# A new order of the pieces of a step, a one-lane last layer and a split output half in a two-layer recurrent kernel

## The chip, the cores and the metric

One core of one Trainium2 chip runs the whole program. The metric is device time in microseconds (us), lower is better. Engines: PE is TensorE's matmuls, PEld its weight loads, DVE VectorE, ACT ScalarE, SP the queue that issues weight DMAs. A "step" below is one pass of the kernel's main loop. The "granted clock" is the share of TensorE's full clock that the profile reports as granted: 1.00 is full, 0.50 half.

## The reference, cut to what matters

```python
def _A_ref(x, mem0, Wq, Wk, Wv, Wo, seg_len):       # 32 heads of 192, model width 640
    mem = mem0                                       # 8 memory rows
    for s in range(n_seg):                           # 64 segments of 32 rows
        h = concat([mem, x[segment s]])              # 40 rows
        q, k, v = h @ Wq, h @ Wk, h @ Wv
        o = softmax(mask(q k^T * scale)) v @ Wo
        mem = o[:, :8]                               # feeds the next segment
        outs.append(o[:, 8:])
def _B_ref(x, wqkv, wo):                             # local attention, 32 heads of 20, window 8, dilation 2
    ...
x = x + A(layernorm(x)); x = x + B(layernorm(x))     # and the same two layers once more
x = x + A(layernorm(x)); x = x + B(layernorm(x))
```

Layer A is recurrent: the memory rows of a segment must be there before the projections of the next one can be made.

## The kernel before

The kernel runs segment t of the first A layer (lane 0) and segment t-2 of the second A layer (lane 1) side by side, so a matmul has 2 x 40 = 80 columns. Steps 0 and 1 have only lane 0, steps 2 to 63 both, steps 64 and 65 only lane 1. Layer B of the step before is woven in. After the last step the list `LAST` does layer B of the last rows alone.

`ORDER` is the order of the pieces in a step. Each engine takes its own pieces in that order. What the argument needs: `K Q V` projections, `S` scores, `E` their exponential (ScalarE), `EM` their mask (VectorE), `PO` attention output in PSUM, `R` reciprocal sums (ScalarE), `OT1 OT2` normalised outputs (VectorE), `Oa Ob` halves of the output projection, `O7x/y/z` the eighth one in three parts; the digit is the quad of heads. `by byE` end layer B and write the next step's input. `LSQ` (VectorE: a square, two reductions, a high and a low part), `lst` (two statistics matmuls), `LMV LR LAP` are the next step's layernorm, `MEMa MEMb` copy the memory rows.

```python
ORDER = """
K0 Q0 bsq K0y QE0 KE0 V0 bst bmv VE0 Q1 S0 K1 T0 QE1 br bap E0 ...
... by byE R5 K7 KE7 V7 S7 VE7 OT15 E7 OT25 LSQ PO6 EM7 Oa2 R6 T7 Ob2 Oa3 TE7
Ob3 OT16 OT26 Oa5 PO7 Oa6 R7 lst LMV Ob5 Oa4 Ob6 OT17 LR OT27 Ob4 LAP O7x O7y MEMa O7z MEMb X1
""".split()
LAST = """
bsq bst bmv br bap bq bqE bk bkE bs0 be0 bv bs1 be1 eb0 bvE bt eb1 btE bp0 on0 bp1 on1 bo boE by byE
""".split()

    def ln_sq(self, x):                                                     # LSQ and bsq
        sq = self.bp.tile([P, NC, NX], BF16, name="sq", tag="sq")
        nc.vector.tensor_tensor(out=sq[:], in0=x[:], in1=x[:], op=ALU.mult)
        s = self.bp.tile([P, 2, NX], F32, name="ln_s", tag="xc")
        for j, v in enumerate((x, sq)):
            nc.vector.tensor_reduce(out=s[:, j, :], in_=v[:].rearrange("p c n -> p n c"), op=ALU.add, ...)
        hl = ...                                                            # part of sq
        nc.vector.tensor_copy(out=hl[:, 0], in_=s[:])
        nc.vector.tensor_tensor(out=hl[:, 1], in0=s[:], in1=hl[:, 0], op=ALU.subtract)
        return hl

    def ln_stats(self, hl):                                                 # lst and bst
        for j in range(2):
            nc.tensor.matmul(ps[:, 0:2 * NX], lhsT=self.ones[:], rhs=hl[:, j]..., start=(j == 0), stop=(j == 1))

    def ln_big(self, x, mr, dst):                                           # LAP and bap
        nc.vector.tensor_tensor(out=xc[:], in0=x[:], in1=m..., op=ALU.subtract)
        for l in range(2):
            nc.vector.tensor_tensor(out=dst[:, :, l, :], in0=xc[...], in1=r..., op=ALU.mult)

    def b_proj(self, part, name):                                           # bq and bk: 64 columns, two lanes
        for n in range(NC):
            for c in range(NC):
                nc.tensor.matmul(ps[:, NX * n:NX * (n + 1)], lhsT=self.wqkv[:, part, c, P * n:P * (n + 1)], rhs=h[:, c, :], ...)
```

The softmax here doesn't subtract the row's maximum and nothing guards it: scores larger than these inputs give would overflow.

Of the kernel before, what the change touches and what calls it, by code (L numbers as in the profile page):

```python
# [12 lines left out]
ACT = mybir.ActivationFunctionType  # L13
ALU = mybir.AluOpType
# [3 lines left out]
P = 128  # L18
# [26 lines left out]


ORDER = """
K0 Q0 bsq K0y QE0 KE0 V0 bst bmv VE0 Q1 S0 K1 T0 QE1 br bap E0 TE0 KE1 V1 S1 EM0 Q3 PO0 VE1 QE3 E1 bq T1 R0 K2
KE2 bqE TE1 Q2 K3 V2 QE2 OT10 S2 KE3 bk EM1 OT20 S3 PO1 VE2 E2 bkE Q4 T2 EM2 bs1 E3 QE4 V3 R1 K4 TE2 be1 VE3
Q5 OT11 OT21 KE4 PO2 R2 EM3 T3 eb1 bs0 be0 V4 QE5 Oa0 VE4 bv TE3 OT12 OT22 bvE Q6 S4 PO3 eb0 E4 bt R3 QE6 btE  # L50
K5 T4 EM4 K6 KE5 TE4 bp0 V5 OT13 Ob0 OT23 KE6 on0 S5 bp1 VE5 PO4 T5 Oa1 E5 R4 on1 TE5 V6 bo Q7 EM5 OT14 S6 boE
OT24 VE6 Ob1 E6 QE7 PO5 T6 EM6 TE6 by byE R5 K7 KE7 V7 S7 VE7 OT15 E7 OT25 LSQ PO6 EM7 Oa2 R6 T7 Ob2 Oa3 TE7
Ob3 OT16 OT26 Oa5 PO7 Oa6 R7 lst LMV Ob5 Oa4 Ob6 OT17 LR OT27 Ob4 LAP O7x O7y MEMa O7z MEMb X1
""".split()


LAST = """
bsq bst bmv br bap bq bqE bk bkE bs0 be0 bv bs1 be1 eb0 bvE bt eb1 btE bp0 on0 bp1 on1 bo boE by byE
""".split()

def half_order():

    order = []
    for n in ORDER:
        if n[0] in "KQV" and len(n) == 2:
            order += [(n[0].lower(), int(n[1]), 0), (n[0].lower(), int(n[1]), 1)]
        elif n[:2] in ("Oa", "Ob"):
            order.append(("o", int(n[2]), int(n[1] == "b")))
        elif n == "O7x":
            order += [("o", 7, 0), ("o", 7, 1)]  # L70
    assert len(set(order)) == len(order) == 8 * NQUAD
    return order

def half_blocks(kind, i, h):

    if kind == "o":
        if i == NQUAD - 1:
            blocks = [(m, c) for c in range(NC) for m in O_ROWS[0] + O_ROWS[1]]
        else:
            blocks = [(m, c) for rows in O_ROWS for m in rows for c in range(NC)]  # L80
    elif (kind, i) == ("k", 0):
        blocks = [(c, n) for c in range(NC - 1) for n in range(6)] + [(NC - 1, n) for n in range(6)]
    else:
        blocks = [(c, n) for n in range(6) for c in range(NC)]
    return blocks[15 * h:15 * (h + 1)]
# [4 lines left out]
def resident_pieces():  # L90

    at, t = {}, 0.0
    for n in ORDER:
        if n[0] in "KQV" and len(n) == 2 and n != "K0":
            at.update({(n[0].lower(), int(n[1]), h): t + 15 * h for h in range(2)})
        elif n == "K0":
            at.update({("k", 0, h): t + 15 * h for h in range(2)})
        elif n[:2] in ("Oa", "Ob"):
            at[("o", int(n[2]), int(n[1] == "b"))] = t
        elif n == "O7x":  # L100
            at.update({("o", 7, h): t + 15 * h for h in range(2)})
        t += 30 if len(n) == 2 and n[0] in "KQV" else 15 if n[0] == "O" and n[1] in "ab" else 30 if n == "O7x" else NO_WEIGHTS.get(n.rstrip("01234567"), 0)
    pieces = [(at[u] + 8 * q, u + (q,)) for u in half_order() for q in range(2)]
    pieces.sort()
    stream, n_s = set(), len(pieces) - N_RES
    k = 0
    for j in range(n_s):
        want = (j + 0.5) * t / n_s
        while k < len(pieces) - (n_s - j) and abs(pieces[k + 1][0] - want) <= abs(pieces[k][0] - want):
            k += 1  # L110
        stream.add(pieces[k][1])
        k += 1
    return {u for _, u in pieces} - stream

class Kernel:
    def __init__(self, ctx, tc, xT, m0T, wA, wqkv, wo, out):

        self.tc = tc
        self.nc = tc.nc
        self.x = xT  # L120
        self.mem0 = m0T
        self.wA = wA
        self.b_src = (wqkv, wo)
        self.out = out
        self.n_seg = 2 * xT.shape[0]
        pool = lambda name, bufs, **kw: ctx.enter_context(tc.tile_pool(name=name, bufs=bufs, **kw))
        self.cp = pool("consts", 1)
        self.wres = pool("wres", 1)
        self.wring = pool("wring", RING)
        self.ap1 = pool("act1", 1)  # L130
        self.ap2 = pool("act2", 2)
        self.bp = pool("bact", 1)
        self.xp = pool("xio", 1)
        self.ps_one = pool("ps_one", 1, space=PSUM)
        self.units = {}
        self.place = {u: n for n, u in enumerate(half_order())}
        self.resident = resident_pieces()
        self.cur = {}
        self.n_big = 0
        self.xt, self.ots, self.qxs, self.kp, self.qp, self.vp, self.tp = {}, {}, {}, {}, {}, {}, {}  # L140
        self.x_load(0)
        self.build_consts()
# [148 lines left out]
    def span_of(self, t):  # L291

        self.l0 = 0 if t < self.n_seg else 1
        self.l1 = 2 if t >= LAG else 1
        self.cs = slice(LT * self.l0, LT * self.l1)

    def proj(self, ps, kind, i, h, t, chained=False):

# [131 lines left out]
    def a_o7(self, part):  # L430

        for k in {"x": range(18), "y": range(18, 24), "z": range(24, 30)}[part]:
            self.o_mm(NQUAD - 1, k // 15, k % 15)

    def acc_lanes(self, g):

        return self.acc[g][:, 0:(3 - g) * NT].rearrange("p (c l n) -> p c l n", l=2, n=LT)
# [18 lines left out]
    def ln_sq(self, x):  # L456

        nc = self.nc
        sq = self.bp.tile([P, NC, NX], BF16, name="sq", tag="sq")
        nc.vector.tensor_tensor(out=sq[:], in0=x[:], in1=x[:], op=ALU.mult)  # L460
        s = self.bp.tile([P, 2, NX], F32, name="ln_s", tag="xc")
        for j, v in enumerate((x, sq)):
            nc.vector.tensor_reduce(out=s[:, j, :], in_=v[:].rearrange("p c n -> p n c"), op=ALU.add, axis=mybir.AxisListType.X)
        hl = sq[:].rearrange("p c n -> p (c n)")[:, 0:4 * NX].rearrange("p (j a n) -> p j a n", j=2, a=2)
        nc.vector.tensor_copy(out=hl[:, 0], in_=s[:])
        nc.vector.tensor_tensor(out=hl[:, 1], in0=s[:], in1=hl[:, 0], op=ALU.subtract)
        return hl

    def ln_stats(self, hl):
        nc = self.nc  # L470
        ps = self.big("ps_st")
        for j in range(2):
            nc.tensor.matmul(ps[:, 0:2 * NX], lhsT=self.ones[:], rhs=hl[:, j].rearrange("p a n -> p (a n)"), start=(j == 0), stop=(j == 1))  # L473
        return ps

    def ln_mv(self, ps):

        nc = self.nc
        m = self.bp.tile([P, NX], F32, name="ln_m")
        nc.vector.tensor_scalar(out=m[:], in0=ps[:, 0:NX], scalar1=1.0 / D, scalar2=None, op0=ALU.mult)  # L480
        v = self.bp.tile([P, NX], F32, name="ln_v")
        nc.vector.tensor_tensor(out=v[:], in0=m[:], in1=m[:], op=ALU.mult)
        nc.vector.scalar_tensor_tensor(out=v[:], in0=ps[:, NX:2 * NX], scalar=1.0 / D, in1=v[:], op0=ALU.mult, op1=ALU.subtract)
        return m, v

    def ln_r(self, mv):

        nc = self.nc
        m, v = mv
        nc.scalar.activation(out=v[:], in_=v[:], func=ACT.Ln, bias=self.eps_t[:])  # L490
        r = self.bp.tile([P, NX], F32, name="ln_r")
        nc.scalar.activation(out=r[:], in_=v[:], func=ACT.Exp, scale=-0.5)
        return m, r

    def ln_big(self, x, mr, dst):
# [1 line left out]
        nc = self.nc  # L497
        m, r = mr
        xc = self.bp.tile([P, NC, NX], F32, name="ln_xc", tag="xc")
        nc.vector.tensor_tensor(out=xc[:], in0=x[:], in1=m[:].unsqueeze(1).to_broadcast([P, NC, NX]), op=ALU.subtract)  # L500
        for l in range(2):
            nc.vector.tensor_tensor(out=dst[:, :, l, :], in0=xc[:, :, SEG * l:SEG * (l + 1)],
                                    in1=r[:, SEG * l:SEG * (l + 1)].unsqueeze(1).to_broadcast([P, NC, SEG]), op=ALU.mult)

# [22 lines left out]
    def b_kE(self, b):  # L527

        o = SEG * (b % 2)
        for l in range(2):  # L530
            k = self.bkp[:, 0:NC * NX].rearrange("p (c l n) -> p l c n", c=NC, l=2)[:, l]
            self.nc.vector.tensor_tensor(out=self.KX[:, :, l, :, o:o + SEG], in0=k.unsqueeze(2).to_broadcast([P, NC, 2, SEG]),
                                         in1=self.par_mask[:].unsqueeze(3).to_broadcast([P, NC, 2, SEG]), op=ALU.mult)
# [1 line left out]
    def b_qE(self):  # L535

        self.qx = self.bp.tile([P, NC, BPC, NX], BF16, name="QX", tag="xc")
        q = self.bqp[:, 0:NC * NX].rearrange("p (c n) -> p c n", c=NC)
        self.nc.vector.tensor_tensor(out=self.qx[:], in0=q.unsqueeze(2).to_broadcast([P, NC, BPC, NX]),
                                     in1=self.pair_mask[:].unsqueeze(3).to_broadcast([P, NC, BPC, NX]), op=ALU.mult)  # L540

    def b_v(self):
        nc = self.nc
# [195 lines left out]
    def a_piece(self, n, t):  # L739
        if n == "K0":  # L740
            return self.k0(t)
        if n == "K0y":
            return self.k0y()
        if n[:2] == "O7":
            return self.a_o7(n[2])
        if n == "X1":
            return self.b_x1(t)
        k, i = n[:-1], int(n[-1])
# [12 lines left out]
    def step(self, t):  # L761
# [3 lines left out]
        nt = t + 1  # L765
        if a:
            self.span_of(t)
        if 1 < nt < self.n_seg:
            self.x_take(nt)
        for n in ORDER if a else LAST:  # L770
# [82 lines left out]
```

## Time and profile before

| stage (profiled run, 3138.8 us) | us |
|---|---|
| start to the end of step 0 | 89.9 |
| step 1 | 48.2 |
| steps 2 to 63, two lanes | 2890.2 |
| shortest / median of these | 46.43 / 46.44 |
| step 64; step 65 up to the last output matmul | 43.7; 45.9 |
| tail: start of the last output matmul to the end of the last sum | 18.4 |
| landing of the output | 2.6 |

A step is counted from the start of its first key matmul to that of the next step. Two-lane steps are 92% of the time.

The busy times by window (each engine's busy us, its instructions in brackets, then TensorE's granted clock, the DMA share and GB/s) in the middle of the run, kernel before:

```profile
core 0: us, PE busy (x) PEld busy (x) DVE busy (x) ACT busy (x) POOL busy (x), PEclk, DMA share, GB/s
1500.00:1600.00 100.00, 99.93 (x2721) 99.59 (x2718) 77.33 (x220) 57.13 (x123) 0.83 (x2) 1.00 0.86 264
```

The timeline of VectorE in the kernel before, around the pieces that make the statistics (columns: start, busy us, engine, line, operation, out<-in, shapes, count):

```profile
1529.21 0.33 DVE L460 TENSOR_TENSOR sq<-xin_86 128x320 bf16<-128x320 bf16 x1
1529.46 0.70 DVE L463 TENSOR_REDUCE ln_s<-xin_86 128x64 f32<-128x320 bf16 x1
1530.08 0.70 DVE L463 TENSOR_REDUCE ln_s<-sq 128x64 f32<-128x320 bf16 x1
1530.81 0.23 DVE L465 CAST sq<-ln_s 128x128 bf16<-128x128 f32 x1
1531.08 0.29 DVE L466 TENSOR_TENSOR sq<-ln_s,sq 128x128 bf16<-128x128 f32 x1
...
1536.29 0.49 DVE L500 TENSOR_TENSOR ln_xc<-xin_86,ln_m 128x320 f32<-128x320 bf16 x1
1536.88 0.56 DVE L502 TENSOR_TENSOR hT_90<-ln_xc,ln_r 128x160 bf16<-128x160 f32 x2
1537.36 0.20 DVE L454 CAST hT_90<-ps_acc_51495 128x48 bf16<-128x48 f32 x1
```

LSQ is the five operations from 1529.21 to 1531.37. The timeline of TensorE in the same kernel:

```profile
1534.09 0.28 PE L473 MATMUL ps_st<-sq,ones 128*128 128x128 bf16 x2
...
1537.17 0.42 PE L420 MATMUL ps_acc_51496<-OT,w_o_11_1962 128*128 128x80 bf16 x7
1537.61 0.45 PE L303 MATMUL ps_k<-hT_90,w_k_00_386 128*128 128x80 bf16 x8
```

The statistics matmuls come 2.7 us after their operands.

The chain of waits of the kernel before in the tail (start, length, engine, tile, line, count):

```profile
3122.83 1.51 PE ps_bq L523 x25
...
3124.36 1.49 DVE QX L539
3125.85 0.41 DVE KX_373 L532
...
3126.30 0.47 PE ps_bs L575 x5
...
3126.79 0.59 ACT EB_142 L581
```

Three further exponentials of 0.59 us follow. Everything in this stretch is serial.

### The profile page before, as it was taken

How to read it: one execution, taken by the hardware profiler on the slowest of the kernel's cores; microseconds unless marked ns; L12 is line 12 of the kernel's file. 1: busy time of each engine (PE TensorE's matmuls, PEld its weight loads, DVE VectorE, ACT ScalarE, POOL GpSimd, SP SyncE). 2: the span in 40 equal slices, each digit the busy share in tenths (PEclk: the TensorE clock that was granted, in tenths of full speed). 3: DMA queues.
4: the chain of work that ended last, by engine and by line, in shares of the span. 5: the costliest groups of instructions: out<-in, count | busy, mean ns of one | idle time of the engine just before them, and what ended most of it. 6: DMA issues, size and time to landing. Idle time of an engine off the chain costs nothing.

```text
span 3138.8 us, 185804 instructions
## 1 busy us (share of the span) xinstructions
PE 3063.2 (98%) x83160; PEld 3036.4 (97%) x83160; DVE 2358.2 (75%) x6883; ACT 1747.2 (56%) x3829; POOL 48.2 (2%) x162
## 2 busy tenths in 40 slices
PE   6899999999999999999999999999999999999996
PEld 5799999999999999999999999999999999999996
DVE  3577777777777777777777777777777777777775
ACT  2355556555556556556555655555655655655653
POOL 2000000000000000000000000000000000000000
PEclk6899999999999999999999999999999999999998
DMA  9988888888888888888888888888888888888885
GB/s 360 320 263 267 263 262 265 264 264 265 266 268 263 268 266 263 268 266 263 268 266 261 267 263 267 261 265 268 263 267 266 264 267 267 263 269 266 262 274 184
DMA packets 487807, 838.02 MB, mean 267 GB/s; under 512 B 54240, under 2 KB 261984, under 8 KB 487008
## 3 DMA queue, kind: packets, MB, share of 16 engines
q1 hardware_dynamic: 477648, 820.89, 83.2%
q8 instruction: 651, 10.67, 1.4%
q10 hardware_dynamic: 9360, 5.26, 0.6%
q14 instruction: 148, 1.21, 0.1%
HBM read 823.31 MB, written 2.62 MB: 263 GB/s over the span
## 4 chain that ended last, share of the span: by engine, by line
PE 95%; DMA 3%; issue 1%; DVE 1%; ACT 0%; SPq 0%; DVEq 0%; ACTq 0%
PE ps_k L303 18%; PE ps_q L303 18%; PE ps_v L303 18%; PE ps_vt L349 6%; PE ps_o L401 5%; PE ps_s L368 5%; PE ps_by L634 2%; PE ps_bq L523 2%; PE ps_bv L548 2%; PE ps_bk L523 2%; DMA w_ring<-in_wA_dram 1%; PE ps_bs L575 1%; PE ps_bo L598 1%; PE ps_bvt L561 1%; PE ps_st L473 0%
## 5 line engine op out<-in xcount | busy, mean ns | idle before, releaser
L303 PEld LDWEIGHTS <-w_ring 128*128 128x128 bf16 x17754 | 784.4, 100 | 19.4 <-DMA w_ring<-in_wA_dram 10.5
L388 ACT ACTIVATE R<-ps_o 64x320 f32<-64x320 f32 (+1 forms) x1056 | 448.5, 425 | 273.8 <-PE ps_o L401 223.6
L342 ACT CAST VT_140<-ps_v 128x480 bf16<-128x480 f32 (+1 forms) x528 | 288.9, 547 | 230.7 <-PE ps_v L303 227.6
L329 ACT CAST KF_121<-ps_k 128x480 bf16<-128x480 f32 (+1 forms) x264 | 144.1, 546 | 391.2 <-PE ps_k L303 383.3
L374 ACT ACTIVATE Em<-ps_s 80x320 bf16<-80x320 f32 (+1 forms) x528 | 223.3, 423 | 157.2 <-PE ps_s L368 110.7
L420 PEld LDWEIGHTS <-w_ring 128*128 128x128 bf16 x6600 | 291.2, 100 | 3.5 <-DMA w_ring<-in_wA_dram 2.6
L335 DVE CAST QT_127<-ps_q 128x320 bf16<-128x320 f32 (+1 forms) x264 | 127.1, 481 | 203.4 <-PE ps_q L303 203.4
L357 DVE COPY Vt_134<-ps_vt 80x512 bf16<-80x512 bf16 x528 | 219.2, 415 | 71.5 <-PE ps_vt L349 69.3
L349 PE MATMUL ps_vt<-ident,VT_140 128*128 128x128 bf16 x3168 | 267.7, 221 | 0.0
L408 DVE TENSOR_TENSOR OT<-ps_o,R 128x320 bf16<-128x320 f32 (+1 forms) x528 | 249.9, 473 | 22.3 <-ACT R L390 16.6
L329 ACT CAST KF_123<-ps_k 128x480 bf16<-128x480 f32 (+1 forms) x264 | 144.1, 546 | 205.6 <-PE ps_k L303 203.9
L390 ACT ACTIVATE R<-R 128x320 f32<-128x320 f32 (+1 forms) x528 | 244.0, 462 | 16.6
L401 PE MATMUL ps_o<-Em,Vt_134 80*128 80x80 bf16 (+1 forms) x4224 | 238.0, 199 | 1.4 <-issue 1.3
L335 DVE CAST QT_125<-ps_q 128x320 bf16<-128x320 f32 (+1 forms) x264 | 126.5, 479 | 143.1 <-PE ps_q L303 71.9
L349 PEld LDWEIGHTS <-VT_140 128*128 128x128 bf16 x3168 | 191.5, 99 | 0.1
L303 PE MATMUL ps_q<-hT_92,w_ring 128*128 128x80 bf16 (+1 forms) x3234 | 185.8, 201 | 3.7 <-DMA w_ring<-in_wA_dram 2.6
L303 PE MATMUL ps_q<-hT_90,w_ring 128*128 128x80 bf16 (+1 forms) x3234 | 186.3, 201 | 2.2 <-DMA w_ring<-in_wA_dram 1.5
L401 PEld LDWEIGHTS <-Vt_134 80*128 80x128 bf16 x4224 | 181.6, 98 | 1.0 <-issue 0.7
L303 PE MATMUL ps_k<-hT_90,w_ring 128*128 128x80 bf16 (+1 forms) x3003 | 172.7, 201 | 1.4 <-DMA w_ring<-in_wA_dram 0.7
L303 PE MATMUL ps_k<-hT_92,w_ring 128*128 128x80 bf16 (+1 forms) x3003 | 171.8, 201 | 1.4 <-issue 1.4
L380 DVE TENSOR_TENSOR Em<-Em,maskA 80x320 bf16<-80x320 bf16 (+1 forms) x528 | 163.2, 309 | 12.5 <-ACT Em L374 8.4
L414 DVE TENSOR_TENSOR OT<-ps_o,R 64x160 bf16<-64x160 f32 (+1 forms) x528 | 165.1, 313 | 7.3
(3084 smaller groups left out, 8305.2 us busy)
## 6 DMA issues: line engine op xcount, KB each, us to landing
w_ring<-in_wA_dram SPq DMA_DIRECT2D x1716, 256.0 KB, 3.9
w_ring<-in_wA_dram SPq DMA_DIRECT2D x1518, 224.0 KB, 4.0
out_dram<-YT_94 ACTq DMA_DIRECT2D x32, 80.0 KB, 3.7
wqkv_sb<-in_wqkv_dram SPq DMA_DIRECT2D x3, 800.0 KB, 7.7
wo_sb<-in_wo_dram SPq DMA_DIRECT2D x1, 800.0 KB, 7.4
w_k_00_386<-in_wA_dram SPq DMA_DIRECT2D x1, 256.0 KB, 2.8
w_k_10_405<-in_wA_dram SPq DMA_DIRECT2D x1, 256.0 KB, 3.8
w_q_10_438<-in_wA_dram SPq DMA_DIRECT2D x1, 256.0 KB, 4.6
```

The lines of the kernel that those rows point to most:

```text
L303: self.nc.tensor.matmul(ps[:, NT * n + c0:NT * n + c1], lhsT=self.block(kind, i, h, k), rhs=hT[:, NT * c + c0:NT * c + c1], start=(h == 0 ...
L329: self.nc.scalar.copy(out=kf[:, :, self.cs], in_=self.kp[i][:, 0:6 * NT].rearrange("p (a n) -> p a n", a=6)[:, :, self.cs])
L335: nc.vector.tensor_copy(out=qt[:, :, 0:4:3, cs], in_=pv[:, :, 0:3:2, cs])
L342: self.nc.scalar.copy(out=vt[:, :, self.cs], in_=self.vp[i][:, 0:6 * NT].rearrange("p (a n) -> p a n", a=6)[:, :, self.cs])
L349: nc.tensor.transpose(out=ps[:, n, :], in_=self.VT[:, NT * n:NT * n + P], identity=self.ident[:])
L357: nc.vector.tensor_copy(out=vt[:, :, 0:4:3, :], in_=src[:, :, 0:3:2, :])
L374: self.nc.scalar.activation(out=e[0:NT, :, cs], in_=self.sv[i][0:NT, :, cs], func=ACT.Exp, scale=float(DH) ** -0.5)
L388: self.nc.scalar.activation(out=r[rows, :, :, self.cs], in_=d, func=ACT.Ln)
L390: self.nc.scalar.activation(out=rf, in_=rf, func=ACT.Exp, scale=-1.0)
L401: nc.tensor.matmul(ov[:, pr, b, self.cs], lhsT=vt[0:NT, 512 * pr + P * b:512 * pr + P * (b + 1)], rhs=em[0:NT, 2 * pr + b // 2, self.cs], ...
L408: self.nc.vector.tensor_tensor(out=ot[:, :, 0:3:2, cs], in0=self.ov[:, :, 0:4:3, cs], in1=self.r[i][:, :, :, cs], op=ALU.mult)
L420: self.nc.tensor.matmul(self.acc[c // 3][:, o:o + self.cs.stop - self.cs.start], lhsT=self.block("o", i, h, k), rhs=ot[:, m, self.cs], sta ...
```

## The change

Intent: layer B of the last rows is needed for one lane only, so its operations at the end are halved; the order of the pieces is new throughout; the seventh quad's second output half is sorted by column and split into `O6x` (nine matmuls) and `O6y` (six, just before `O7x`).

```diff
-... LSQ PO6 EM7 Oa2 R6 T7 Ob2 Oa3 TE7
-Ob3 OT16 OT26 Oa5 PO7 Oa6 R7 lst LMV Ob5 Oa4 Ob6 OT17 LR OT27 Ob4 LAP O7x O7y MEMa O7z MEMb X1
+... K7 TE7 Ob2 by QE7 KE7 OT16 S7 E7 OT26 byE
+EM7 Oa5 Oa3 PO7 Oa4 LSQ Ob3 lst Oa6 O6x R7 Ob4 LMV LR OT17 Ob5 OT27 O6y O7x O7y O7z LAP MEMa MEMb X1
 (the rest of ORDER is new too; cut)
 LAST = """
-bsq bst bmv br bap bq bqE bk bkE bs0 be0 bv bs1 be1 eb0 bvE bt eb1 btE bp0 on0 bp1 on1 bo boE by byE
+bsq bst bmv br bap bk bkE bq bqE bv bs1 be1 bvE eb1 bt btE bp0 on0 bp1 on1 bo boE by byE
@@ half_blocks
+            if i == NQUAD - 2:
+                blocks = blocks[:15] + sorted(blocks[15:], key=lambda b: b[1])
@@ ln_sq, ln_stats, ln_mv, ln_r, ln_big, b_kE, b_qE: slices by lane
+        ns = self.b_rows()
-        nc.vector.tensor_tensor(out=sq[:], in0=x[:], in1=x[:], op=ALU.mult)
+        nc.vector.tensor_tensor(out=sq[:, :, ns], in0=x[:, :, ns], in1=x[:, :, ns], op=ALU.mult)
 (the others alike; cut)
@@ step
         if a:
             self.span_of(t)
+        else:
+            self.bl = range(1, 2)
```

More of the change, by code (lines that the diff above doesn't have):

```diff
@@ L47 @@
 ORDER = """
-K0 Q0 bsq K0y QE0 KE0 V0 bst bmv VE0 Q1 S0 K1 T0 QE1 br bap E0 TE0 KE1 V1 S1 EM0 Q3 PO0 VE1 QE3 E1 bq T1 R0 K2
-KE2 bqE TE1 Q2 K3 V2 QE2 OT10 S2 KE3 bk EM1 OT20 S3 PO1 VE2 E2 bkE Q4 T2 EM2 bs1 E3 QE4 V3 R1 K4 TE2 be1 VE3
-Q5 OT11 OT21 KE4 PO2 R2 EM3 T3 eb1 bs0 be0 V4 QE5 Oa0 VE4 bv TE3 OT12 OT22 bvE Q6 S4 PO3 eb0 E4 bt R3 QE6 btE
-K5 T4 EM4 K6 KE5 TE4 bp0 V5 OT13 Ob0 OT23 KE6 on0 S5 bp1 VE5 PO4 T5 Oa1 E5 R4 on1 TE5 V6 bo Q7 EM5 OT14 S6 boE
-OT24 VE6 Ob1 E6 QE7 PO5 T6 EM6 TE6 by byE R5 K7 KE7 V7 S7 VE7 OT15 E7 OT25 LSQ PO6 EM7 Oa2 R6 T7 Ob2 Oa3 TE7
-Ob3 OT16 OT26 Oa5 PO7 Oa6 R7 lst LMV Ob5 Oa4 Ob6 OT17 LR OT27 Ob4 LAP O7x O7y MEMa O7z MEMb X1
+K0 K0y Q0 bsq V0 KE0 QE0 VE0 bst Q1 bmv br S0 K1 K2 QE1 E0 KE1 T0 bap KE2 EM0 TE0 S1 bq V1 bk bqE PO0 E1 Q2
+VE1 T1 bkE bs0 QE2 R0 K3 V2 TE1 be0 EM1 OT10 Q3 KE3 OT20 S2 VE2 E2 PO1 T2 V3 R1 QE3 TE2 bs1 eb0 OT11 S3 K4 VE3
+be1 OT21 Q4 T3 E3 KE4 EM2 PO2 R2 QE4 EM3 V4 S4 VE4 Q5 TE3 OT12 OT22 V5 QE5 E4 T4 PO3 EM4 K5 VE5 Oa0 eb1 bv TE4
+R3 OT13 KE5 Q6 bvE S5 OT23 E5 bt PO4 QE6 T5 Ob0 EM5 btE TE5 K6 bp0 R4 KE6 OT14 OT24 V6 S6 bp1 Oa2 VE6 on0 E6
+PO5 on1 T6 Oa1 Ob1 bo EM6 TE6 R5 OT15 V7 boE OT25 Q7 PO6 VE7 T7 R6 K7 TE7 Ob2 by QE7 KE7 OT16 S7 E7 OT26 byE
+EM7 Oa5 Oa3 PO7 Oa4 LSQ Ob3 lst Oa6 O6x R7 Ob4 LMV LR OT17 Ob5 OT27 O6y O7x O7y O7z LAP MEMa MEMb X1
 """.split()
 LAST = """
-bsq bst bmv br bap bq bqE bk bkE bs0 be0 bv bs1 be1 eb0 bvE bt eb1 btE bp0 on0 bp1 on1 bo boE by byE
+bsq bst bmv br bap bk bkE bq bqE bv bs1 be1 bvE eb1 bt btE bp0 on0 bp1 on1 bo boE by byE
 """.split()
@@ L68, in half_order @@
             order.append(("o", int(n[2]), int(n[1] == "b")))
+        elif n == "O6x":
+            order.append(("o", 6, 1))
         elif n == "O7x":
@@ L99, in resident_pieces @@
             at[("o", int(n[2]), int(n[1] == "b"))] = t
+        elif n == "O6x":
+            at[("o", 6, 1)] = t
         elif n == "O7x":
             at.update({("o", 7, h): t + 15 * h for h in range(2)})
-        t += 30 if len(n) == 2 and n[0] in "KQV" else 15 if n[0] == "O" and n[1] in "ab" else 30 if n == "O7x" else NO_WEIGHTS.get(n.rstrip("01234567"), 0)
+        t += 30 if len(n) == 2 and n[0] in "KQV" else 15 if n[0] == "O" and n[1] in "ab" else 30 if n == "O7x" else 15 if n == "O6x" else NO_WEIGHTS.get(n.rstrip("01234567"), 0)
     pieces = [(at[u] + 8 * q, u + (q,)) for u in half_order() for q in range(2)]
@@ L139, in __init__ @@
         self.n_big = 0
+        self.bl = range(2)
         self.xt, self.ots, self.qxs, self.kp, self.qp, self.vp, self.tp = {}, {}, {}, {}, {}, {}, {}
@@ L295, in span_of @@
         self.cs = slice(LT * self.l0, LT * self.l1)
+        self.bl = range(2)
     def proj(self, ps, kind, i, h, t, chained=False):
@@ L433, in a_o7, with a_o6 @@
             self.o_mm(NQUAD - 1, k // 15, k % 15)
+    def a_o6(self, part):
+        for k in {"x": range(9), "y": range(9, 15)}[part]:
+            self.o_mm(NQUAD - 2, 1, k)
     def acc_lanes(self, g):
@@ L459, in ln_sq @@
         sq = self.bp.tile([P, NC, NX], BF16, name="sq", tag="sq")
-        nc.vector.tensor_tensor(out=sq[:], in0=x[:], in1=x[:], op=ALU.mult)
+        ns = self.b_rows()
+        nc.vector.tensor_tensor(out=sq[:, :, ns], in0=x[:, :, ns], in1=x[:, :, ns], op=ALU.mult)
         s = self.bp.tile([P, 2, NX], F32, name="ln_s", tag="xc")
         for j, v in enumerate((x, sq)):
-            nc.vector.tensor_reduce(out=s[:, j, :], in_=v[:].rearrange("p c n -> p n c"), op=ALU.add, axis=mybir.AxisListType.X)
+            nc.vector.tensor_reduce(out=s[:, j, ns], in_=v[:, :, ns].rearrange("p c n -> p n c"), op=ALU.add, axis=mybir.AxisListType.X)
         hl = sq[:].rearrange("p c n -> p (c n)")[:, 0:4 * NX].rearrange("p (j a n) -> p j a n", j=2, a=2)
-        nc.vector.tensor_copy(out=hl[:, 0], in_=s[:])
-        nc.vector.tensor_tensor(out=hl[:, 1], in0=s[:], in1=hl[:, 0], op=ALU.subtract)
+        nc.vector.tensor_copy(out=hl[:, 0, :, ns], in_=s[:, :, ns])
+        nc.vector.tensor_tensor(out=hl[:, 1, :, ns], in0=s[:, :, ns], in1=hl[:, 0, :, ns], op=ALU.subtract)
         return hl
@@ L472, in ln_stats @@
         for j in range(2):
-            nc.tensor.matmul(ps[:, 0:2 * NX], lhsT=self.ones[:], rhs=hl[:, j].rearrange("p a n -> p (a n)"), start=(j == 0), stop=(j == 1))
+            nc.tensor.matmul(ps[:, 0:2 * NX].rearrange("p (a n) -> p a n", a=2)[:, :, self.b_rows()], lhsT=self.ones[:], rhs=hl[:, j, :, self.b_rows()],
+                             start=(j == 0), stop=(j == 1))
         return ps
@@ L478, in ln_mv @@
         nc = self.nc
+        ns = self.b_rows()
         m = self.bp.tile([P, NX], F32, name="ln_m")
-        nc.vector.tensor_scalar(out=m[:], in0=ps[:, 0:NX], scalar1=1.0 / D, scalar2=None, op0=ALU.mult)
+        nc.vector.tensor_scalar(out=m[:, ns], in0=ps[:, ns], scalar1=1.0 / D, scalar2=None, op0=ALU.mult)
         v = self.bp.tile([P, NX], F32, name="ln_v")
-        nc.vector.tensor_tensor(out=v[:], in0=m[:], in1=m[:], op=ALU.mult)
-        nc.vector.scalar_tensor_tensor(out=v[:], in0=ps[:, NX:2 * NX], scalar=1.0 / D, in1=v[:], op0=ALU.mult, op1=ALU.subtract)
+        nc.vector.tensor_tensor(out=v[:, ns], in0=m[:, ns], in1=m[:, ns], op=ALU.mult)
+        nc.vector.scalar_tensor_tensor(out=v[:, ns], in0=ps[:, NX + ns.start:NX + ns.stop], scalar=1.0 / D, in1=v[:, ns], op0=ALU.mult, op1=ALU.subtract)
         return m, v
@@ L489, in ln_r @@
         m, v = mv
-        nc.scalar.activation(out=v[:], in_=v[:], func=ACT.Ln, bias=self.eps_t[:])
+        ns = self.b_rows()
+        nc.scalar.activation(out=v[:, ns], in_=v[:, ns], func=ACT.Ln, bias=self.eps_t[:])
         r = self.bp.tile([P, NX], F32, name="ln_r")
-        nc.scalar.activation(out=r[:], in_=v[:], func=ACT.Exp, scale=-0.5)
+        nc.scalar.activation(out=r[:, ns], in_=v[:, ns], func=ACT.Exp, scale=-0.5)
         return m, r
@@ L499, in ln_big @@
         xc = self.bp.tile([P, NC, NX], F32, name="ln_xc", tag="xc")
-        nc.vector.tensor_tensor(out=xc[:], in0=x[:], in1=m[:].unsqueeze(1).to_broadcast([P, NC, NX]), op=ALU.subtract)
-        for l in range(2):
+        ns = self.b_rows()
+        nc.vector.tensor_tensor(out=xc[:, :, ns], in0=x[:, :, ns], in1=m[:, ns].unsqueeze(1).to_broadcast([P, NC, ns.stop - ns.start]), op=ALU.subtract)
+        for l in self.bl:
             nc.vector.tensor_tensor(out=dst[:, :, l, :], in0=xc[:, :, SEG * l:SEG * (l + 1)],
@@ L529, in b_kE @@
         o = SEG * (b % 2)
-        for l in range(2):
+        for l in self.bl:
             k = self.bkp[:, 0:NC * NX].rearrange("p (c l n) -> p l c n", c=NC, l=2)[:, l]
@@ L537, in b_qE, with b_rows @@
         self.qx = self.bp.tile([P, NC, BPC, NX], BF16, name="QX", tag="xc")
-        q = self.bqp[:, 0:NC * NX].rearrange("p (c n) -> p c n", c=NC)
-        self.nc.vector.tensor_tensor(out=self.qx[:], in0=q.unsqueeze(2).to_broadcast([P, NC, BPC, NX]),
-                                     in1=self.pair_mask[:].unsqueeze(3).to_broadcast([P, NC, BPC, NX]), op=ALU.mult)
+        ns = self.b_rows()
+        w = ns.stop - ns.start
+        q = self.bqp[:, 0:NC * NX].rearrange("p (c n) -> p c n", c=NC)[:, :, ns]
+        self.nc.vector.tensor_tensor(out=self.qx[:, :, :, ns], in0=q.unsqueeze(2).to_broadcast([P, NC, BPC, w]),
+                                     in1=self.pair_mask[:].unsqueeze(3).to_broadcast([P, NC, BPC, w]), op=ALU.mult)
+    def b_rows(self):
+        return slice(SEG * self.bl[0], SEG * (self.bl[-1] + 1))
     def b_v(self):
@@ L743, in a_piece @@
             return self.k0y()
-        if n[:2] == "O7":
-            return self.a_o7(n[2])
+        if n[:2] in ("O6", "O7"):
+            return self.a_o7(n[2]) if n[1] == "7" else self.a_o6(n[2])
         if n == "X1":
```

## The prediction

> **What bounds it now.** The 62 two-lane steps are TensorE-bound. In the window 1500 to 1600 us TensorE is busy 99.93%, VectorE 77%, ScalarE 57%, DMA 86%, clock 1.00. In the timeline, from one step's first key matmul to the next takes 46.43 us in the undisturbed steps, and the chain of waits there is nothing but matmuls: 30 projection matmuls of 80 columns take 1.073 to 1.078 us, 35.8 ns each. That agrees with the Trainium skill, "TensorE: Matmul & The Clock Gate", section "Back-to-back issue gap" (80/2.4 + 2.5 = 35.8 ns). So 62 x 46.43 = 2879 us is a floor that a new order cannot lower. The same steps really take 2890 us: about 11 us of stalls, mostly late weights (list of waits: 10.5 us of weight loads behind the ring's DMA). The rest: 90 us of first step (DMA-bound), 48 us second step, 44 + 45 us single-lane steps at the end (gaps named "issue"), and from 3118 us a tail of about 18 us plus the output's landing.
>
> **What the change does.**
> 1. Tail on one lane. The chain of waits there: two reductions 1.21 us, the small statistics operations, ps_bq 1.51, QX 1.49, KX 0.41, four exponentials 4 x 0.59, the rest unhalved. Halving: reductions and other layernorm about -0.9 us; q/k projection and expansions about -0.5 to -1.5 (bv, unhalved, now stands before bs1); two exponentials -1.2. Estimate: -3 us, all of it on the critical path.
> 2. New order in all steps. No matmul added or removed, so it can only add or remove stalls. I counted, with the trace's durations, the TensorE work between each producer and its consumer. Almost everywhere the slack stays. One place does not: the statistics matmuls of the next step's layernorm. Before, their five VectorE operations (1529.21 to 1531.37, 2.16 us) end 2.9 us before the matmuls at 1534.25. After, they stand behind the mask of the eighth quad's scores (EM7), and the matmuls (lst) come soon after. From the end of scores S7: exponential 0.2+0.43, mask 0.25, then 2.16, hand-over 0.05: about 3.1 us. TensorE has only Oa5, Oa3, PO7, Oa4, Ob3 in between: 4 x 0.54 + 0.29 = 2.45 us. VectorE and TensorE's matmuls keep program order (same page, section on the 16 sub-arrays, queue depths), so TensorE waits 0.55 to 0.63 us in each step: about +36 us over 62 steps, +1 in the single-lane ones.
> 3. Splitting the seventh quad's second output half: the end of the step (last softmax to output to memory rows) keeps 2.15 us of matmuls between the statistics and the last outputs, so no gain and no loss there.
> 4. The pause lets the weight DMA catch up: estimate -6 us of the 11 us of late weights.
>
> Sum: 3143 + 36 + 1 - 3 - 6 = about 3170; I say 3168 us. Range 3134 to 3184. Chances: faster by over 2% 0.01, within 2% 0.95, slower by over 2% 0.04.
>
> **What would show it.** Undisturbed steps of about 47.0 us instead of 46.43; the list of waits with a new entry of ps_st (or its weight load) on VectorE's sq (L465/L466 of before), about 0.3 us each, some 30 to 38 us in all; TensorE busy share down by a point; the tail from the last x1 sum to the last output sum 15 us instead of 18; other TensorE waits unchanged.
>
> **What would make it wrong.** If the layernorm operations start before EM7 ends or are shorter, step 2's 36 us vanishes and the time is about 3137. A second stall I overlooked (score buffers, shared PSUM rotation), or new weight stalls from different resident pieces, would add. The half-clock stretch at the start or in the single-lane steps may shift by several us.

On its first citation: that section gives the formula for isolated matmuls, and 81 ns at 128 columns for a stream in which each matmul has its own weight load. Here each has its own (2721 matmuls, 2718 weight loads in the 100 us above), and yet the formula fits: 35.8 ns at 80 columns, and 56 ns at 128 in the transposes (`ps_vt`).

## The result, and the profile after

The kernel before took 3141.27 us (median of 4 runs, 3138.91 to 3145.83), the changed one 3172.84 us (median of 4, 3170.09 to 3174.21). The ratio is 1.0098 with a 95% interval of 1.008 to 1.0115. A ratio here is the mean time of one kernel's fast runs over that of the other's of the same rounds, so it is not quite the ratio of the medians quoted.

Where the 33.7 us between the two profiled runs lie (same stages as above):

| stage | before | after | difference |
|---|---|---|---|
| to the end of step 0 | 89.9 | 89.7 | -0.1 |
| step 1 | 48.2 | 51.5 | +3.4 |
| steps 2 to 63 | 2890.2 | 2923.6 | +33.4 |
| shortest two-lane step | 46.43 | 46.97 | +0.54 |
| step 64 | 43.7 | 44.6 | +0.9 |
| step 65 to the last output matmul | 45.9 | 43.7 | -2.2 |
| tail | 18.4 | 16.8 | -1.6 |

62 times 0.54 is 33.5. Step 1 and the tail ran at different granted clocks before and after; this is taken up below. The busy times by window in the middle of the changed kernel:

```profile
1500.00:1600.00 100.00, 98.81 (x2663) 97.77 (x2661) 77.17 (x224) 56.52 (x122) 0.82 (x2) 1.00 0.86 262
```

TensorE made 2663 matmuls in 100 us instead of 2721. The timeline of the changed kernel, all engines, from the eighth quad's scores to the statistics (the bracket at a line's end names what its engine waited for):

```profile
1548.45 0.45 PE L376 MATMUL ps_s<-QT_127,KF_123 128*128 128x160 bf16 x6
...
1548.93 0.43 ACT L382 ACTIVATE Em<-ps_s 80x320 bf16<-80x320 f32 x1 [0.95 <-PE ps_s L376]
1549.07 0.33 DVE L668 TENSOR_TENSOR xin_86<-ps_by,x_369 128x160 bf16<-128x160 f32 x1
...
1549.31 0.32 DVE L671 TENSOR_TENSOR YT_94<-ps_by,x_369 128x160 bf16<-128x160 f32 x1
...
1549.54 0.31 DVE L388 TENSOR_TENSOR Em<-Em,maskA 80x320 bf16<-80x320 bf16 x1
...
1549.77 0.32 DVE L474 TENSOR_TENSOR sq<-xin_86 128x320 bf16<-128x320 bf16 x1
...
1550.01 0.70 DVE L477 TENSOR_REDUCE ln_s<-xin_86 128x64 f32<-128x320 bf16 x1
...
1551.21 0.24 PE L428 MATMUL ps_acc_51600<-OT,w_ring 128*128 128x80 bf16 x2
1551.36 0.23 DVE L479 CAST sq<-ln_s 128x128 bf16<-128x128 f32 x1
...
1551.62 0.29 DVE L480 TENSOR_TENSOR sq<-ln_s,sq 128x128 bf16<-128x128 f32 x1
1551.64 0.54 PE L487 MATMUL ps_st<-sq,ones 128*128 128x128 bf16 x2 [0.20 <-DVE sq L479]
1552.02 0.27 PE L428 MATMUL ps_acc_51599<-OT,w_o_00_1837 128*128 128x80 bf16 x3
```

LSQ now starts at 1549.77, behind the mask at 1549.54 and the two sums of byE (1549.07 and 1549.31), the first of which makes its input. The two output matmuls at 1551.21 are the last work that TensorE has; without a wait the statistics would start at 1551.28 and the next output matmul about 0.11 us later. The first statistics matmul starts when the high part of 1551.36 is ready, the second when the low part of 1551.62 is ready, and the next output matmul starts at 1552.02: about 0.6 us late. In the regular steps the statistics cost 0.63 us; the distance before the eighth quad's attention output (`ps_o`) grew from 0.07 to 0.14 us, and the one between the last output matmul and the next keys shrank from 0.23 us to 0.07. Together that is the 0.54 us by which the step is longer.

The list of waits in the two-lane steps of the changed kernel (us in total, times, longest), TensorE's matmuls:

```profile
PE ps_st L487 <- DVE sq L479: 12.2, 61, 0.2
```

and its weight loads, which run ahead of the matmuls:

```profile
PEld L487 <- DVE sq L479: 20.5, 62, 0.3
PEld L428 <- issue: 13.9, 64, 0.4
```

The second of these is, once in each step, the load for the output matmuls behind the statistics. The same list of the kernel before has no wait for sq, and 1.0 us of "issue" at the output projection (L420 there); its largest entry is:

```profile
PEld L303 <- issue: 5.8, 17, 0.9
```

The 12.2 us are only 0.20 per step, since the matmul's record before it covers the rest of the pause. The start times give the true size. (The prediction expected 30 to 38 us in this list.)

The chain of waits in the tail of the changed kernel:

```profile
3156.96 1.52 PE ps_bk L541 x25
3158.48 1.33 PE ps_bq L541 x25
3159.81 1.33 PE ps_bv L572 x25
3161.14 0.55 PE ps_bs L599 x5
3161.72 0.59 ACT EB_142 L605
3162.32 0.59 ACT EB_142 L605
3162.93 0.43 ACT VTB_378 L579
```

Two exponentials are gone, but three whole projections now stand in line before the scores.

### The profile page after: what moved, and what is told of

Same layout as the page of the kernel before. It is cut to its first block, busy times and chain, and to the rows that moved or that the text cites. A ratio compares the mean times of both kernels' runs of the same rounds, so it can differ in the third digit from the quotient of the medians.

```text
span 3172.5 us, 186182 instructions
## 1 busy us (share of the span) xinstructions
PE 3082.6 (97%) x83155; PEld 3041.9 (96%) x83155; DVE 2361.4 (74%) x6880; ACT 1757.3 (55%) x3827; POOL 48.2 (2%) x162
## 4 chain that ended last, share of the span: by engine, by line
PE 83%; DVE 8%; ACT 4%; DMA 3%; issue 2%; SPq 0%; ACTq 0%; DVEq 0%
PE ps_q L311 17%; PE ps_v L311 17%; PE ps_k L311 15%; PE ps_vt L357 5%; PE ps_o L409 4%; PE ps_s L376 4%; DVE ln_s L477 3%; ACT R L396 2%; PE ps_bk L541 2%; PE ps_bq L541 2%; PE ps_bv L572 2%; DMA w_ring<-in_wA_dram 1%; PE ps_bs L599 1%; ACT KF_123 L337 1%; DVE OT L416 1%
## 5 line engine op out<-in xcount | busy, mean ns | idle before, releaser
L337 ACT CAST KF_121<-ps_k 128x480 bf16<-128x480 f32 (+1 forms) x264 | 143.3, 543 | 272.2 <-PE ps_k L311 272.2
L311 PE MATMUL ps_q<-hT_92,w_ring 128*128 128x80 bf16 (+1 forms) x3498 | 200.4, 201 | 5.5 <-issue 3.8
L311 PE MATMUL ps_q<-hT_90,w_ring 128*128 128x80 bf16 (+1 forms) x3498 | 201.2, 201 | 4.0 <-issue 1.8
L311 PE MATMUL ps_k<-hT_90,w_ring 128*128 128x80 bf16 (+1 forms) x3234 | 185.7, 201 | 2.5 <-DMA w_ring<-in_wA_dram 1.8
L311 PE MATMUL ps_k<-hT_92,w_ring 128*128 128x80 bf16 (+1 forms) x3234 | 185.8, 201 | 1.5 <-issue 1.5
L605 ACT ACTIVATE EB_142<-ps_bs 64x512 bf16<-64x512 f32 x262 | 154.8, 591 | 32.1 <-PE ps_bs L599 29.0
```

The source lines that it names most:

```text
L311: self.nc.tensor.matmul(ps[:, NT * n + c0:NT * n + c1], lhsT=self.block(kind, i, h, k), rhs=hT[:, NT * c + c0:NT * c + c1], start=(h == 0 ...
L337: self.nc.scalar.copy(out=kf[:, :, self.cs], in_=self.kp[i][:, 0:6 * NT].rearrange("p (a n) -> p a n", a=6)[:, :, self.cs])
```

## The experiments

Ten kernels ran. All results were correct unless said. Theory: TensorE waits in each step for LSQ, which the new order of VectorE has put behind EM7. Rivals: A, the one-lane code costs time in all steps; B, the split output half delays the step's end; C, other causes such as other resident weights; D, only the place of the statistics matmuls is wrong. The step lengths are from each kernel's profiled run. In lsq_long, lst_early and lst_late the shortest step is a single one, the first with two lanes; there the median is the regular step (most of the 62 lie within 0.02 us of it), and the text below goes by it.

| run | shortest (median) two-lane step, us | time, us | before, same chip | ratio (95%) |
|---|---|---|---|---|
| lane_only | 46.43 (46.44) | 3135.61 | 3138.53 | 0.9991 (0.9978 to 1.0005) |
| order_only | 46.96 (46.97) | 3169.87 | 3138.53 | 1.01 (1.0086 to 1.0114) |
| split_only | 46.43 (46.44) | 3138.01 | 3138.53 | 1.0 (0.9986 to 1.0013) |
| lsq_short | 46.34 (46.35) | 3128.55 | 3133.28 | 0.9984 (0.9969 to 0.9999) |
| lsq_long | 47.21 (47.33) | 3186.02 | 3133.28 | 1.0175 (1.0158 to 1.0192) |
| before_lsq_long | 46.67 (46.69) | 3148.97 | 3133.28 | 1.0046 (1.0032 to 1.0061) |
| lst_early | 47.07 (47.14) | 3177.18 | 3133.28 | 1.0137 (1.0122 to 1.0152) |
| lst_late | 47.10 (47.20) | 3181.51 | 3139.17 | 1.0139 (1.0124 to 1.0155) |
| best_tail | 46.43 (46.44) | 3132.28 | 3138.53 | 0.9982 (0.997 to 0.9995) |
| best_center | 46.28 (46.28) | 3125.01 | 3139.17 | 0.9957 (0.9944 to 0.9969) |

### The three parts of the change, one at a time

```diff
 lane_only: the changed kernel
-ORDER (new)
+ORDER (of before)
-            if i == NQUAD - 2: blocks = ... sorted ...
```

> Kernel before with the last rows' local layer on one lane and its new order at the end, but the old order of all steps. Theory (the loss is a wait of the layernorm statistics matmuls made by the new order of the steps; the tail gains a little): undisturbed two-lane steps stay at 46.43 us; the tail from the end of the last output matmuls to the last output sum is 16.5 us as in the changed kernel, against 18.2 before; so 1 to 4 us less than before, ratio 0.9987 to 0.9997. Rival A (the one-lane code itself costs time in every step): steps near 46.97, ratio about 1.01.

Measured: steps as before, so rival A falls. The tail took 15.7 us by the definition of the table above. That is 1.1 us less than in the changed kernel, which was not expected: the tail's code is the same. What differs is the granted clock. In the changed kernel it was 0.50 from 3156.18 on, before `ps_bk` at 3156.96 (1.52 us); in lane_only it fell only at 3120.22, and the chain of waits there has

```profile
3119.38 0.89 PE ps_bk L539 x25
```

The total is 0.1% lower with an interval that includes 1: at this size the gain is seen in the tail of the profile, not in the total time.

```diff
 order_only: the changed kernel
-LAST (new)
+LAST (of before)
-        else:
-            self.bl = range(1, 2)
```

> Changed kernel with its new order and split output half, but the last rows' layer on two lanes in the old order at the end. Theory: steps 46.97 us, the statistics matmuls wait about 0.55 us in each, total 1 to 3 us above the changed kernel, ratio to before 1.010 to 1.012. Rival A (one-lane code costs): steps 46.43, ratio 0.999 to 1.001.

Measured: steps of 46.96 us and 1% more time: the new order alone carries the loss. Its profiled tail is 19.3 us against the changed kernel's 16.8 (and 18.4 in the kernel before, with the same tail code but a clock of 1.00 from 3126.01 to 3129.42, over `ps_bv`); in the total that difference is not seen (ratio 1.01 against 1.0098, from separate calls).

```diff
 split_only: the kernel before, two lanes in LAST
+            if i == NQUAD - 2: blocks = ... sorted ...
-... Ob5 Oa4 Ob6 OT17 LR OT27 Ob4 LAP O7x ...
+... Ob5 Oa4 O6x OT17 LR OT27 Ob4 LAP O6y O7x ...
```

> Kernel before with only the seventh quad's second output half split: nine matmuls of its first three columns where the half stood, six just before the eighth quad's. Theory: steps 46.43 to 46.5 us, ratio 0.999 to 1.001. Rival B (the split delays the end of the step): steps near 46.97, ratio about 1.01, with the wait at the start of the next step's keys.

Measured: no change at all. Rival B falls, and the split neither helps nor hurts by itself.

### Is it LSQ, and by how much?

```diff
 lsq_short: the changed kernel, LSQ only (wrong result on purpose)
-in_=v[:, :, ns].rearrange("p c n -> p n c")
+in_=v[:, 0:1 if probe else NC, ns].rearrange("p c n -> p n c")
```

> Changed kernel, with the two reductions of the layernorm operations before the statistics matmuls taken over one of five chunks only (wrong result on purpose). One reduction falls from 0.62 to about 0.2 us, so these operations end about 0.85 us earlier. Theory (TensorE waits for the end of these operations, 0.54 us a step): the wait vanishes, steps 46.43 to 46.5 us, ratio to before 0.998 to 1.001. Rival C (the cost is elsewhere: other resident weights, instruction supply, PSUM turns): steps stay near 46.97, ratio 1.01.

Measured: the result is wrong (relative error 0.027), and with the same order, weights and matmuls the step falls by 0.63 us to 46.34. Rival C falls as the cause of the 0.54 us. That 46.34 is below the kernel before was not expected: the statistics no longer wait, while the shorter distance before the next keys (0.07 us against 0.23) stays. It is taken up under best_center.

```diff
 lsq_long: the changed kernel; before_lsq_long: the kernel before
-        nc.vector.tensor_tensor(out=sq..., in0=x..., in1=x..., op=ALU.mult)
+        for _ in range(2 if probe else 1):
+            nc.vector.tensor_tensor(out=sq..., in0=x..., in1=x..., op=ALU.mult)
```

> Changed kernel, with the squaring among these operations done twice (0.24 us more on VectorE). Theory: all of it shows, steps 47.2 us, ratio to before about 1.015. Rival C: steps stay near 46.97.

> The same doubled squaring in the kernel before. There the statistics matmuls have 2.9 us of slack, but VectorE runs without a pause from these operations to the sixth-index quad's outputs, and the next attention output (ps_o) waits about 0.04 us for those: theory, steps 46.6 to 46.7 us with a wait of ps_o, none of ps_st. If VectorE had slack there: 46.43.

Measured: the second squaring costs 0.36 us and not 0.24. VectorE and TensorE in a regular step of lsq_long:

```profile
938.57 0.68 DVE L475 TENSOR_TENSOR sq<-xin 128x320 bf16<-128x320 bf16 x2
...
939.16 0.71 DVE L478 TENSOR_REDUCE ln_s<-xin 128x64 f32<-128x320 bf16 x1
...
940.80 0.54 PE L488 MATMUL ps_st<-sq,ones 128*128 128x128 bf16 x2 [0.56 <-DVE sq L480]
```

From the squaring to the first reduction it is 0.59 us instead of 0.24. In the changed kernel all of that shows: the distance before the first statistics matmul grows from 0.40 to 0.76 us and the regular step by 0.35 us (46.98 to 47.33). Over 62 steps that is 22 us; the total grew by about 24 (ratio 1.0098 to 1.0175, against 1.015 expected). Only one step of the 62, at 47.21 us, fits the expectation. In the kernel before the same extra work costs 0.25 us (46.44 to 46.69): the distance between the starts of the last output matmul before it and the next attention output (`ps_o`) grows from 0.07 us to 0.32. So the kernel before had much slack at its statistics, but only about 0.1 us in VectorE's queue behind LSQ: a pause before OT16, which shrank from 0.295 to 0.198 us between starts. VectorE at 77% busy was otherwise on the critical path of that stretch.

### Is such a wait enough by itself?

```diff
 lst_early: the kernel before
-... Oa2 R6 T7 ... R7 lst LMV ...
+... Oa2 lst R6 T7 ... R7 LMV ...
```

> Kernel before with only the two statistics matmuls moved earlier in TensorE's order, right behind Oa2, where the trace of before puts TensorE at 1530.90 us and the end of their operands at 1531.37. Theory (such a wait alone is enough for the loss): they wait about 0.47 us, steps 46.85 to 46.95 us, ratio about 1.009 to 1.011. Rivals B and C (split or weights): steps 46.43, ratio 1.000.

Measured: more than expected, 47.14 us instead of 46.85 to 46.95. The wait itself is 0.63 us, not 0.47: I had taken the end of Oa2 from the chain of waits, which counts a matmul's latency, while TensorE can start the next one about 0.17 us sooner. The timeline of lst_early on TensorE shows it:

```profile
1689.60 0.42 PE L420 MATMUL ps_acc<-OT,w_o 128*128 128x80 bf16 x7
1690.21 0.54 PE L473 MATMUL ps_st<-sq,ones 128*128 128x128 bf16 x2 [0.20 <-DVE sq L465]
1690.59 0.50 PE L349 MATMUL ps_vt<-ident,VT 128*128 128x128 bf16 x6
```

Seven matmuls from 1689.60 at 36 ns end their starts at 1689.82; the statistics come at 1690.21. The pause also holds back T7 behind it, and the distance before the next step's keys grows from 0.23 to 0.34 us. Moving only these two matmuls in the kernel before thus gives a loss of the same kind, and a larger one: 0.70 us in a step against 0.54.

### Would moving the statistics cure it?

```diff
 lst_late: the changed kernel
-... LSQ Ob3 lst Oa6 O6x R7 Ob4 LMV ...
+... LSQ Ob3 Oa6 O6x lst R7 Ob4 LMV ...
```

> Changed kernel with the statistics matmuls moved 0.86 us later in TensorE's order (behind Oa6 and O6x), so that they no longer wait. Theory (not this wait alone, but VectorE's chain from the masked scores through these operations to the memory rows sets the step's end): the statistics then come 0.18 us later for VectorE, the last outputs wait about 0.5 us for OT27 instead, and the next keys for the memory rows; steps about 47.15 us, a little worse than the changed kernel's 46.97. Rival D (only the place of this wait was wrong): steps 46.43 to 46.5.

Measured: worse, 47.20 us against 46.98. The wait at the statistics is gone and stands at two other places, as the list of waits of lst_late in the two-lane steps shows:

```profile
PE ps_acc L428 <- DVE OT L422: 15.0, 60, 0.3
PE ps_k L311 <- DVE hT L467: 13.2, 60, 0.6
```

Rival D falls for this place; no other place was tried. The statistics are where the loss shows. What makes it, as lsq_short and this run together indicate, is that in the new order VectorE's chain, from OT16 and OT26 over byE, EM7 and LSQ to the last outputs and the memory rows, is longer than the matmuls set beside it: in the timeline of the changed kernel (shown in part above) VectorE has no pause from OT16 at 1547.99 to the end of LSQ at 1551.91.

### A version better than both

```diff
 best_tail: lane_only, and
 b_proj, b_v, b_wo:
-ps[:, NX * n:NX * (n + 1)], ... rhs=h[:, c, :]
+ps[:, NX * n + ns.start:NX * n + ns.stop], ... rhs=h[:, c, ns]
 LAST:
-... bqE bv bs1 be1 bvE ...
+... bqE bs1 bv be1 bvE ...
 (b_vE also on one lane)
```

> lane_only, with the tail's projections (bk, bq, bv, by) also on one lane (32 columns instead of 64) and bs1 placed before bv. Theory: in the changed kernel's tail bk, bq, bv and by took 1.52, 1.33, 1.33 and 1.51 us at half clock; 32 columns should take 0.7 to 0.9 each, and bs1 waits for QX (0.8) instead of bv (1.3): tail about 14 us instead of 16.5 and 18.2, steps at 46.43, ratio to before about 0.9985. If weight loads bound these matmuls, they stay near 1.3 us and the tail is about 16 us.

Measured: a tail of 14.3 us. The chain of waits of best_tail there:

```profile
3117.44 0.82 PE ps_bk L539 x25
3118.26 0.68 PE ps_bq L539 x25
...
3118.97 0.84 DVE QX L557
...
3119.85 0.71 PE ps_bs L599 x5
```

From ps_bk to ps_bs it is 2.41 us instead of 4.18. 25 matmuls of 32 columns in 0.68 us are 27 ns each.

```diff
 best_center: best_tail, and
-... PO7 Oa6 R7 lst LMV ...
+... PO7 lst Oa6 R7 LMV LXC ...
 (LXC is the first operation of LAP, x minus mean, taken out of LAP)
```

> best_tail, with the centring of the next step's layernorm taken out of its end and put, with earlier statistics matmuls, in VectorE's pause before the last outputs. Shortening these operations in the changed kernel gave steps of 46.34 us, 0.09 below the kernel before: theory, VectorE's 0.5 us of centring between OT27 and the memory rows holds up the next step's keys by 0.09 us in the kernel before too. Then steps are 46.34 us and the total 5 to 6 us below best_tail, ratio to before about 0.996. If the accumulators' end is what the keys wait for, steps stay at 46.43 and the ratio at 0.998.

Measured: 0.43% faster than before, and steps of 46.28 us, lower still than expected. Its VectorE timeline at the end of a step, against that of the kernel before shown above (1536.29 to 1537.36):

```profile
1668.23 0.48 DVE L687 TENSOR_TENSOR ln_xc<-xin,ln_m 128x320 f32<-128x320 bf16 x1
1668.92 0.49 DVE L414 TENSOR_TENSOR OT<-ps_o,R 128x320 bf16<-128x320 f32 x1 [0.21 <-ACT R L396]
...
1669.99 0.56 DVE L692 TENSOR_TENSOR hT<-ln_xc,ln_r 128x160 bf16<-128x160 f32 x2
1670.90 0.21 DVE L465 CAST hT<-ps_acc 128x48 bf16<-128x48 f32 x1 [0.35 <-PE ps_acc L426]
```

The centring stands in a pause before the last outputs. The copy of the memory rows (1670.90), which in the kernel before began as soon as VectorE was free, now waits 0.35 us for the accumulator, and the pause between the last output matmul and the next keys is gone. The two edits (earlier statistics, earlier centring) were made together, so their shares are not told apart.

## Why the prediction was right or wrong

- **The new wait: right, the sum of it with some luck.** "TensorE waits 0.55 to 0.63 us in each step: about +36 us over 62 steps". The statistics cost 0.63 us and the 62 steps grew by 33.4. order_only puts it on the order, lsq_short on LSQ, lst_early shows that such a wait suffices, and lsq_long gives the slope: 0.36 us more work, 0.35 us more step. The estimate holds because it compared TensorE's work in between (2.45 us) with the durations of one chain on the other engines (3.1 us); the Trainium skill, "TensorE: Matmul & The Clock Gate", section "Step-by-step: what each phase is for", says that matmuls stay in program order (the section that the prediction names says it outright only of VectorE): the output matmuls behind the statistics start at 1552.02, though OT16 and OT26, which they read, were done at 1549.04. The luck: the step grew by only 0.54 us because its end, of which the prediction said "no gain and no loss there", gained 0.16 us before the keys and lost 0.07 at `ps_o`.
- **The cause was told too narrowly.** That the statistics' operations "stand behind the mask of the eighth quad's scores (EM7)" is true, but the mask is the smaller part of what holds them up. The prediction came to it from the scores and their exponential, which ended at 1549.36; the mask started only at 1549.54, when VectorE was done with byE. And going ahead of EM7 could have brought LSQ forward by at most the mask's 0.23 us (an estimate from 1549.54 and 1549.77; no run tried it), since LSQ reads what byE writes. lst_late shows that moving the statistics to one later place did not save the time either.
- **The tail: mechanism right, size off.** "Estimate: -3 us" measured -1.6 in the profiled runs. The mis-sized term is "q/k projection and expansions about -0.5 to -1.5": from the first projection to the scores the chain went from 3.47 us (3122.83 to 3126.30) to 4.18 (3156.96 to 3161.14), +0.7. The change does not halve the projections and it sets bv before the scores; that took away the gain, and the granted clock made it a loss: in lane_only, with the same tail code and a later half clock, the same stretch took 3.50 us and the tail was 2.7 us shorter than before. The other terms were right: layernorm -1.2 (predicted -0.9), scores and exponentials with what follows to ps_bvt -1.1 (predicted -1.2). best_tail halves the projections and takes 2.41 us there, -1.1 against before, which is within what was predicted.
- **"The pause lets the weight DMA catch up: estimate -6 us": its premise is wrong, the rest not shown.** The 10.5 us of weight waits in the list of the whole run were read as if they lay in the two-lane steps; they lie in steps 0 and 1 (6.8 and 3.7), and that list restricted to the two-lane steps names no weight DMA, only "issue". The time beyond 62 times the median step was 10.9 us before and 10.7 after, so nothing was caught up in these two profiles. But in the other runs this excess was between 1.9 and 7.7 us, with the old order and with the new (4.8 in order_only), so one profile of each decides little. What causes it is open.
- **"A floor that a new order cannot lower": wrong by 0.15 us.** best_center, with no fewer matmuls in a step, reaches 46.28. The pause before the keys was hidden in the busy share.
- **Step 1** took 3.4 us more in the profiled run of the changed kernel, at a mean granted clock of 0.82 instead of 0.91. Step 1 took 51.4 us in before_lsq_long with the old order and 48.4 in lsq_short with the new, so nothing puts it down to the change.

The prediction's terms add up to 3171 us; 3168 was given, without a reason. That it came near the measured 3172.84 (3174.21 in the profiled run) is partly luck: the catching-up and the tail were taken 7 us too favourably, and step 1 (3.4 us) was not in it, but the main term was 2.6 us too large, the single-lane steps 2.3 (+1 predicted, -1.3 measured), and its base of 3143 us 2.5 (the profiled run of the kernel before took 3140.52).

## What to carry to other kernels

When TensorE is busy all the time, judge a new order by each hand-over: set the matmul time between producer and consumer beside the serial time of the chain on the other engines, queue included, and multiply a shortfall by the number of steps. An engine at 77% can still be the critical one over a stretch of a few us, and then moving the instruction that waits only moves the wait; shorten the chain or start it earlier. Read TensorE's pauses from the distances between matmul starts, and read a wait's place (which stage) before counting on it. Before comparing stretches of a us or two, compare their granted clocks.

## What the Trainium skill lacked or had wrong

- "Perfetto Trace Analysis", section "Identifying the Most-Contended Engine", advises the share of the peak rate (MFU, which was not worked out here) and the weight loads' busy share in place of the matmuls'. Here the weight loads' share too was 99.59% in the kernel before, although best_center still took 0.15 us (0.3%) out of each step; the distances between starts showed it, which that section does not name.
- "TensorE: Matmul & The Clock Gate", section "What's actually happening", lets the clock fall to half after an idle window of about 3.4 us. In the kernel before the granted clock was 0.50 from 3115.76 to 3126.01, and the longest distance between matmul starts in the single-lane steps up to there was 2.1 us (1.8 just before it, at 3115.09). So shorter pauses, several in a row, came before a half clock here. (A later section of the page, on PSUM queues, tells of short idle times that did so in another kernel, but gives no length.)
- No page was found to have the gaps that this profile names "issue". In the two-lane steps of the kernel before, weight loads spent 5.8 us in 17 of them at the projections alone; no run here settled their cause.
